# One PSUM read per tile in the cosine layer, and rounds of part-array matmuls issued as one piece

## The chip, the cores and the metric

The kernel runs on one core of a Trainium2 chip. The metric is device time in microseconds (us) of one execution. TensorE (PE) does matmuls, VectorE (DVE), ScalarE (ACT) and GpSimd (POOL) the elementwise work, and SyncE (SP) issues the transfers between HBM and SBUF. Matmul results land in PSUM, which has 8 banks here: four stand as accumulators, four are a ring that all other matmul results share.

## The reference

Shapes: q, k, v are 8 x 8 x 576 x 64, p is 8 x 8 x 32 x 64, the two layers have d_model 512 and d_ff 2048, and 4608 tokens.

```
def sm_attn(qq, kk, vv):
    s = scale * qq @ kk.T
    a = exp(s - max(s)); a = a / (sum(a) + 1e-9)
    return a @ vv
p_packed = sm_attn(p, k, v)             # per batch and head, 32 packed rows
x = sm_attn(q, p_packed, p_packed)      # then heads side by side: 4608 x 512
h = x @ w_in;   x = (h * cos(h)) @ w_out                       # layer 1
h = x @ w_in2;  out = (h * tanh(softplus(h))) @ w_out2         # layer 2
```

## The kernel before, in words

The program has two stages. Stage 1 (to about 843 us) does the attention and layer 1 together, stage 2 does layer 2 with fewer products (a Strassen-like scheme) and is not touched.

**Layer 1** goes through 256 steps n, a tile of 288 tokens by 128 hidden units each (16 token tiles `t`, 16 hidden tiles `s`). `l1(n)` takes a bank of the ring and does six matmuls into it (`mm3` twice: each product is done as hi*hi, hi*lo, lo*hi, hence lines 145, 146 and 147 of every matmul row). `chain_first(n)` and `chain_cos(n)` make g = h*cos(h); `chain_split(n)` makes g's high part (rounded, L819) and low part (the rest, L822 on POOL); `l2(n)` multiplies them with w_out into four accumulator banks, 12 matmuls. `evac(t)` writes a finished token tile to HBM. The chain reads `st["h"]`, the bank of `l1`, three times: on ACT at L802 (the whole number of turns, written as int32), on DVE at L804 (h minus that many turns) and on DVE at L812 (times h). Between them L805 clamps the angle on DVE and L811 takes the sine on ACT. The bank goes back to the ring when L812 is done.

**The attention** runs beside it as units with stages that a table places at steps: `k_unit` (16 of them, packed keys), `q_unit` (16, one per token tile) and `w_unit` (40, which fold the packed values into w_in). Their matmuls have 32 output columns, so each uses a part of the array: eight of them (L218 in `k_unit.s2_pe`, L351 in `q_unit.s2_pe`, L491 in `w_unit.pe`; there four where a unit has one batch) fill all parts and are called a round here, and `k_unit.s5_pe` (L279) has twenty. An fp32 matmul leaves two records in the trace, so a round of eight shows as x16.

**Order.** Instructions are written step by step, but a list scheduler at build time sets the order on each engine from priorities and a timeline of its own. On the chip an engine takes its instructions in that order, and one that waits holds all behind it. `tc.high_priority(offset=...)` lifts an instruction in the scheduler's queue, `tc.issue_after(ins)` keeps it behind `ins`. Before, `w_unit.pe` alone uses both to pull the rest of a round up behind its first matmul.

Of the kernel before, what the change touches and what calls it, by code (L numbers as in the profile page):

```python
# [8 lines left out]
F32 = mybir.dt.float32  # L9
F32R = mybir.dt.float32r  # L10
I32 = mybir.dt.int32
AF = mybir.ActivationFunctionType
ALU = mybir.AluOpType
AX = mybir.AxisListType

B, H, S, D, NPK = 8, 8, 576, 64, 32
DM, DFF = 512, 2048
NTOK = B * S
TT = 288
# [3 lines left out]
NBT = NTOK // BT  # L23
LAG_A = 3
G_MOD = 2
G_ACT = (0, 1)
C_MOD = 2
C_POOL = ()
W_POS = ((57, 1.1), (55, 1.2), (52, 1.2))
K_LD = 3  # L30
Q_LD = 2
# [22 lines left out]
Q_DVE = (0, 0, 0)  # L54
X2_AT = 231
COMB = 240
STOP = 0
W0E = (-3, 5, -1, 9)
K0_G1 = 1
# [9 lines left out]
HP_W = 400  # L69
# [13 lines left out]
TWO_PI = 2.0 * math.pi  # L83
STEP = [None]
PERM = ((0, 2, 1, 3), (1, 3, 0, 2))


def build(tc, q, k, v, p, w1i, w1o, w2i, w2o, out):
    nc = tc.nc
    ctx = ExitStack()  # L90
    with ctx:
        wpool = ctx.enter_context(tc.tile_pool(name="wpool", bufs=1))
# [5 lines left out]
        def nm(s):  # L98
            cnt[0] += 1
            return f"{s}_{cnt[0]}"  # L100
# [17 lines left out]

        ident = wpool.tile([128, 128], F32, name="ident")
        make_identity(nc, ident)  # L120
        halfpi = wpool.tile([128, 1], F32, name="halfpi")
        nc.vector.memset(halfpi, math.pi / 2)
        quarter = wpool.tile([128, 1], F32, name="quarter")
        nc.vector.memset(quarter, 0.25)
        wpool.tile([128, 8], F32, name="gap_w")
# [6 lines left out]
        ap = apool_cm.__enter__()  # L132
# [22 lines left out]
        def trans2(dst, raw):  # L155
# [2 lines left out]
                bass.AP(raw.tensor, raw.offset, [raw.ap[0], [544, 2], [64, 9], [1, 32]]),  # L158
            )

        PK = {}
        lastexp = [None]

        def k_unit(b, g, alloc_v):
# [16 lines left out]
            def vload(i):  # L181
                def f():
                    r = alloc_v([128, 512])
                    if i < 2:
                        h = 4 * g + 2 * i
                        nc.sync.dma_start(
                            r.rearrange("p (h w) -> p h w", h=2),
                            v[b, h : h + 2, :512, :].rearrange("h (t c) d -> t h (c d)", c=4),
                        )
                    else:  # L190
                        nc.sync.dma_start(
                            r[:64, :256].rearrange("p (h d) -> p h d", d=D),
                            v[b, 4 * g : 4 * g + 4, 512:576, :].rearrange("h s d -> s h d"),
                        )
                    st["vr"].append(r)

                return f
# [14 lines left out]

            def s2_pe():
                st["s1"] = [ring() for _ in range(2)]
                for l in range(4):
                    h = PERM[par][l]
                    for x in range(2):
                        nc.tensor.matmul(  # L218
                            st["s1"][x][32 * l : 32 * l + 32, :TT].rearrange("p (s a) -> p a s", a=9),
                            st["pp"][64 * x : 64 * x + 64, 32 * h : 32 * h + 32],  # L220
                            st["kt"][64 * x : 64 * x + 64, TT * h : TT * h + TT].rearrange("p (a s) -> p a s", s=32),
                            start=True,
                            stop=True,
                        )

            def s2_ew():
                sm = ap.tile([128, 8], F32, tag="sm", bufs=3, name=nm("sm"))
# [20 lines left out]
            def s4_pe():  # L248
                e = st["e"]
                t1, t2 = ring(), ring()  # L250
                ev = e[:, :512].rearrange("p (t c) -> p c t", c=4)
                for c in range(4):
                    nc.tensor.transpose(t1[:, 128 * c : 128 * c + 128], ev[:, c], ident)
                nc.tensor.transpose(t2[:64, :128], e[:, 512:576], ident)
                st["t"] = (t1, t2)

            def s4_ew():
                t1, t2 = st["t"]
                a4 = tmp_tile([128, 512])
                a5 = ap.tile([128, 128], F32, tag="a5", bufs=1, name=nm("a5"))  # L260
                nc.scalar.copy(a4, t1)
                nc.scalar.copy(a5[:64], t2[:64, :128])
                st["a"] = (a4, a5)
                sm = st["sm"]
                nc.vector.tensor_tensor(sm[:, 6:7], sm[:, 4:5], sm[:, 5:6], ALU.add)
                nc.vector.tensor_scalar(sm[:, 6:7], sm[:, 6:7], EPS, None, ALU.add)
                nc.vector.reciprocal(sm[:, 7:8], sm[:, 6:7])

            def s5_pe():
                a4, a5 = st["a"]  # L270
                ps = ring()
                for c in range(5):
                    n = 128 if c < 4 else 64
                    a = a4[:, 128 * c : 128 * c + 128] if c < 4 else a5[:64]
                    for l in range(4):
                        h = PERM[par][l]
                        vr = st["vr"][h // 2] if c < 4 else st["vr"][2]
                        o = 256 * (h % 2) + D * c if c < 4 else D * h
                        nc.tensor.matmul(  # L279
                            ps[32 * l : 32 * l + 32, :D],  # L280
                            a[:, 32 * l : 32 * l + 32],
                            vr[:n, o : o + D],
                            start=c == 0,
                            stop=c == 4,
                        )
                st["pv"] = ps

            def s5_ew():
# [28 lines left out]
        def q_unit(t, pre=None):  # L317
# [27 lines left out]

            def s2_pe():
                st["s"] = [ring() for _ in range(2)]
                for l in range(4):
                    h = PERM[b % 2][l]
                    for g in range(2):  # L350
                        nc.tensor.matmul(  # L351
                            st["s"][g][32 * l : 32 * l + 32, :TT],
                            PK[(b, g)][64 * g : 64 * g + 64, 32 * l : 32 * l + 32],
                            st["kt"][64 * g : 64 * g + 64, TT * h : TT * h + TT],
                            start=True,
                            stop=True,
                        )

            def s2_ew():
                sq = tmp_tile([128, 2, TT])  # L360
# [120 lines left out]
        def w_unit(bs, fg, g, ms):  # L481
            st = {}

            def pe():
                for b in bs:
                    st[b] = ring()

                def head(b, l):
                    h = PERM[b % 2][l]
                    r = 64 * (h % 2)  # L490
                    return nc.tensor.matmul(  # L491
                        st[b][32 * l : 32 * l + 32],
                        PK[(b, g)][r : r + 64, 32 * l : 32 * l + 32],
                        ms[h // 2]["m"][r : r + 64],
                        start=True,
                        stop=True,
                    )

                todo = sorted(((b, l) for b in bs for l in range(4)), key=lambda x: (-(PERM[x[0] % 2][x[1]] // 2), -x[0]))
                ins = head(*todo[0])  # L500
                with tc.issue_after(getattr(ins, "ins", ins)), tc.high_priority(offset=HP_W):
                    for x in todo[1:]:
                        head(*x)

            def ew():
                for b in bs:
                    w = W1.get((b, fg))
                    if w is None:
                        w = W1[(b, fg)] = wab_tile(b % 2, [128, 2, 2, 512], F32R)
                    nc.scalar.copy(w[:, g, 0], st[b])  # L510
                    nc.vector.tensor_tensor(w[:, g, 1], st[b], w[:, g, 0], ALU.subtract)

            return pe, ew
# [284 lines left out]

        def chain_first(n):
            st = hst[n]  # L800
            ki = ap.tile([128, TT], I32, tag="ki", bufs=2, name=nm("ki"))
            nc.scalar.activation(ki, st["h"], AF.Identity, bias=quarter, scale=1.0 / TWO_PI)  # L802
            r = ap.tile([128, TT], F32, tag="r", bufs=4, name=nm("r"))
            nc.vector.scalar_tensor_tensor(r, ki, -TWO_PI, st["h"], ALU.mult, ALU.add)  # L804
            (nc.gpsimd if n % C_MOD in C_POOL else nc.vector).tensor_scalar(r, r, 1.570796, -4.712388, ALU.min, ALU.max)  # L805
            st["r"] = r

        def chain_cos(n):
            st = hst[n]
            g = st["r"]  # L810
            nc.scalar.activation(g, g, AF.Sin, bias=halfpi, scale=1.0)  # L811
            nc.vector.tensor_tensor(g, g, st["h"], ALU.mult)  # L812
            st["g"] = g

        def chain_split(n):
            st = hst[n]
# [20 lines left out]
        def evac(t):  # L837
            for dc in range(4):
                o = ap.tile([128, TT], F32, tag="xo", bufs=3, name=nm("xo"))
                x = acc[t][dc][:, :TT].rearrange("p (a s) -> p s a", s=32)  # L840
                y = o.rearrange("p (s a) -> p s a", s=32)
                if dc % 2 == 0:
                    nc.scalar.copy(y, x)
                else:
                    nc.vector.tensor_copy(y, x)
                nc.sync.dma_start(x2d[t][:, dc, :], o)

        X = {}
# [351 lines left out]
```

## Time and profile before

| | |
|---|---|
| median of 3 runs | 1555.14 us (1553.41 to 1558.32) |
| the profiled execution | 1555.48 us, of which the span of instructions is 1552.9 us |
| PE busy, share of the span | 1475.9 us, 95% |
| DVE, ACT, POOL busy | 72%, 57%, 41% |
| granted PE clock, mean over the span | 0.989 of full speed |

A PE that is busy is not a PE at its peak: matmuls overlap, so what a piece of the matmul stream costs is read from start to start in the timeline, not from busy time. The idle time that a row names stands behind its last bar, with what ended it.

### The profile page before, as it was taken

How to read it: one execution, taken by the hardware profiler on the slowest of the kernel's cores; microseconds unless marked ns; L12 is line 12 of the kernel's file. 1: busy time of each engine (PE TensorE's matmuls, PEld its weight loads, DVE VectorE, ACT ScalarE, POOL GpSimd, SP SyncE). 2: the span in 40 equal slices, each digit the busy share in tenths (PEclk: the TensorE clock that was granted, in tenths of full speed). 3: DMA queues.
4: the chain of work that ended last, by engine and by line, in shares of the span. 5: the costliest groups of instructions: out<-in, count | busy, mean ns of one | idle time of the engine just before them, and what ended most of it. 6: DMA issues, size and time to landing. Idle time of an engine off the chain costs nothing.

```text
span 1552.9 us, 28652 instructions
## 1 busy us (share of the span) xinstructions
PE 1475.9 (95%) x9728; PEld 1278.3 (82%) x9728; DVE 1117.8 (72%) x2082; ACT 883.9 (57%) x1838; POOL 639.2 (41%) x634
## 2 busy tenths in 40 slices
PE   3789999999999999999999999999999999999998
PEld 1567778788987898788999887888889898888997
DVE  4896666777776877678675878678668857766756
ACT  3675767666667677667665455344443534454443
POOL 0462333245643544627754666223522622352102
PEclk9899999999999999999999999999999999999999
DMA  9889676436648457533313767668868877877887
GB/s 293 283 214 226 170 184 161 123 101 176 186 122 225 139 152 195 163 107 104 104 49 98 259 217 241 193 196 242 266 212 235 298 223 219 244 205 221 241 257 202
DMA packets 247377, 300.75 MB, mean 194 GB/s; under 512 B 104384, under 2 KB 129472, under 8 KB 247232
## 3 DMA queue, kind: packets, MB, share of 16 engines
q1 hardware_dynamic: 246432, 298.73, 66.1%
q8 instruction: 77, 1.26, 0.3%
q14 instruction: 68, 0.56, 0.1%
q10 hardware_dynamic: 800, 0.20, 0.1%
HBM read 242.22 MB, written 56.62 MB: 192 GB/s over the span
## 4 chain that ended last, share of the span: by engine, by line
PE 50%; DVE 6%; ACT 3%; issue 2%; DMA 2%; POOL 1%; SPq 0%; DVEq 0%; ACTq 0%; POOLq 0%
PE acc L146 9%; PE acc L147 9%; PE acc L145 9%; PE ps L145 8%; PE ps L147 8%; PE ps L146 8%; DVE r L805 1%; ACT r L811 1%; DVE r L812 1%; DVE r L804 1%; DMA raw<-in_moe_w_in_dram 1%; DVE wab L897 1%; ACT wab L896 1%; PE ps L491 0%; DMA tst<-wt 0%
## 5 line engine op out<-in xcount | busy, mean ns | idle before, releaser
L822 POOL TENSOR_TENSOR gh<-r,gh 128x288 fp32r<-128x288 f32 x256 | 214.9, 847 | 334.3 <-ACT gh L819 231.7
L146 PE MATMUL acc<-gh,wo 128*128 128x288 f32 x1024 | 301.5, 301 | 2.2 <-POOL gh L822 1.7
L147 PE MATMUL acc<-gh,wo 128*128 128x288 f32 x1024 | 298.2, 298 | 0.0
L955 POOL TENSOR_TENSOR gh<-t,gh 128x512 fp32r<-128x512 f32 (+1 forms) x108 | 144.2, 1340 | 351.5 <-ACT gh L954 290.7
L145 PE MATMUL acc<-gh,wo 128*128 128x288 f32 x1024 | 273.7, 304 | 2.1 <-ACT gh L819 1.9
L145 PEld LDWEIGHTS acc<-gh,wo 128*128 128x128 f32 x1024 | 181.2, 190 | 34.6 <-issue 11.9
L146 PE MATMUL acc<-gh,T 128*128 128x512 f32 (+1 forms) x560 | 207.0, 371 | 2.2 <-DVE gh L955 1.7
L145 PE MATMUL ps<-wab,ws 128*128 128x512 f32 (+1 forms) x560 | 206.0, 369 | 1.8 <-ACT gh L954 0.8
L146 PEld LDWEIGHTS acc<-gh,wo 128*128 128x128 f32 x1024 | 194.1, 190 | 15.9 <-issue 9.5
L146 PE MATMUL ps<-wab,ws 128*128 128x512 f32 (+1 forms) x560 | 206.4, 369 | 0.0
L147 PE MATMUL ps<-wab,ws 128*128 128x512 f32 (+1 forms) x560 | 205.4, 369 | 0.0
L147 PE MATMUL acc<-gh,T 128*128 128x512 f32 (+1 forms) x560 | 205.1, 369 | 0.0
L147 PEld LDWEIGHTS acc<-gh,wo 128*128 128x128 f32 x1024 | 194.2, 190 | 5.8 <-issue 5.6
L955 DVE TENSOR_TENSOR gh<-wo,gh 128x512 fp32r<-128x512 f32 (+1 forms) x160 | 128.7, 810 | 81.7 <-ACT gh L954 81.3
L811 ACT ACTIVATE r<-r,halfpi 128x288 f32<-128x288 f32 x256 | 136.3, 535 | 83.9 <-DVE r L805 81.6
L145 PE MATMUL acc<-gh,T 128*128 128x512 f32 (+1 forms) x560 | 181.9, 369 | 0.6 <-DMA T<-tst 0.5
L145 PE MATMUL ps<-aT,wab 128*128 128x288 f32 x512 | 159.7, 312 | 22.7 <-DVE r L812 16.5
L812 DVE TENSOR_TENSOR r<-r,ps 128x288 f32<-128x288 f32 x256 | 114.5, 449 | 73.3 <-ACT r L811 72.5
L802 ACT ACTIVATE ki<-ps,quarter 128x288 int32<-128x288 f32 x256 | 125.1, 496 | 59.7 <-PE ps L147 49.6
L804 DVE SCALAR_TENSOR_TENSOR r<-ki,ps 128x288 f32<-128x288 int32 x256 | 113.8, 447 | 55.8 <-ACT ki L802 39.5
L146 PE MATMUL ps<-aT,wab 128*128 128x288 f32 x512 | 152.2, 297 | 0.0
L147 PE MATMUL ps<-aT,wab 128*128 128x288 f32 x512 | 151.5, 296 | 0.0
(169 smaller groups left out, 2956.1 us busy)
## 6 DMA issues: line engine op xcount, KB each, us to landing
T<-tst SPq DMA_DIRECT2D x280, 256.0 KB, 3.1
ws<-wst SPq DMA_DIRECT2D x224, 256.0 KB, 3.0
ld<-ws SPq DMA_DIRECT2D x80, 256.0 KB, 3.5
kr<-in_k_dram SPq DMA_DIRECT2D x64, 272.0 KB, 5.6
kr<-in_q_dram SPq DMA_DIRECT2D x60, 272.0 KB, 6.0
tst<-wt SPq DMA_DIRECT2D x56, 256.0 KB, 2.6
wst<-ws SPq DMA_DIRECT2D x56, 256.0 KB, 2.5
x2d<-xo SPq DMA_DIRECT2D x64, 144.0 KB, 1.8
```

What stands on the lines that cost most here:

```text
L145: nc.tensor.matmul(ps, l0, r0, start=first, stop=False, skip_group_check=more)
L146: nc.tensor.matmul(ps, l0, r1, start=False, stop=False, skip_group_check=more)
L147: nc.tensor.matmul(ps, l1, r0, start=False, stop=last, skip_group_check=more)
L802: nc.scalar.activation(ki, st["h"], AF.Identity, bias=quarter, scale=1.0 / TWO_PI)
L804: nc.vector.scalar_tensor_tensor(r, ki, -TWO_PI, st["h"], ALU.mult, ALU.add)
L805: (nc.gpsimd if n % C_MOD in C_POOL else nc.vector).tensor_scalar(r, r, 1.570796, -4.712388, ALU.min, ALU.max)
L811: nc.scalar.activation(g, g, AF.Sin, bias=halfpi, scale=1.0)
L812: nc.vector.tensor_tensor(g, g, st["h"], ALU.mult)
L822: nc.gpsimd.tensor_tensor(gh[:, 1], st["g"], gh[:, 0], ALU.subtract)
L896: nc.scalar.copy(x[:, a, 0, :n], src)
L897: (nc.gpsimd if k % 2 == 0 else nc.vector).tensor_tensor(x[:, a, 1, :n], src, x[:, a, 0, :n], ALU.subtract)
L955: eng.tensor_tensor(hl[:, 1, :n], src, hl[:, 0, :n], ALU.subtract)
```

## The change

Three things are changed. In the chain, ACT copies h / 2pi out of PSUM into an SBUF tile `f`; everything after it works on `f` and a second SBUF tile `u` (turns as int32, angle in turns, sine). The clamp is gone, the product is f * sin, and `evac` multiplies by 2pi. The high part is made by ACT at even steps and by DVE at odd ones (`G_ACT`), before by ACT at all. In the rounds, a new helper `rounds` puts a 128x32 matmul (with the identity as weights) on the round's first bank, reading the end of the round's last operand, ahead of the first part-array matmul, and lifts the others behind that. It serves `k_unit.s2_pe`, `q_unit.s2_pe` and those `w_unit.pe` that have two batches; `k_unit.s5_pe` uses it without the short matmul and starts with the block that was last. To that end the small transpose and its copy move from partitions 0 to 63 to 64 to 127.

```diff
-G_ACT = (0, 1)
+G_ACT = (0,)
+HOLD_N = 32
+        def rounds(banks, src, first, rest):
+            for ps in banks:
+                nc.tensor.matmul(ps[:, :HOLD_N], ident, src[:, :HOLD_N], start=True, stop=True)
+            with tc.high_priority(offset=HP_W):
+                ins = first()
+            with tc.issue_after(getattr(ins, "ins", ins)), tc.high_priority(offset=HP_W):
+                for f in rest:
+                    f()
...
+                todo = [lambda x=x, l=l: head(x, l) for x, l in sorted(((x, l) for x in range(2) for l in range(4)), key=lambda y: (-PERM[par][y[1]], -y[0]))]
+                rounds(st["s1"][:1], st["kt"][:, 1152 - HOLD_N :], todo[0], todo[1:])
...
-                nc.tensor.transpose(t2[:64, :128], e[:, 512:576], ident)
+                nc.tensor.transpose(t2[:, :128], e[:, 448:576], ident)
...
-                nc.scalar.copy(a5[:64], t2[:64, :128])
+                nc.scalar.copy(a5[64:], t2[64:, :128])
...
+                todo = [lambda c=c, l=l: head(c, l) for c in (4, 0, 1, 2, 3) for l in range(4)]
+                rounds((), None, todo[0], todo[1:])
...
-                ins = head(*todo[0])
-                with tc.issue_after(getattr(ins, "ins", ins)), tc.high_priority(offset=HP_W):
-                    for x in todo[1:]:
-                        head(*x)
+                rounds([st[b] for b in bs[:-1]], ms[1]["m"], lambda: head(*todo[0]), [lambda x=x: head(*x) for x in todo[1:]])
...
-            ki = ap.tile([128, TT], I32, tag="ki", bufs=2, name=nm("ki"))
-            nc.scalar.activation(ki, st["h"], AF.Identity, bias=quarter, scale=1.0 / TWO_PI)
-            r = ap.tile([128, TT], F32, tag="r", bufs=4, name=nm("r"))
-            nc.vector.scalar_tensor_tensor(r, ki, -TWO_PI, st["h"], ALU.mult, ALU.add)
-            (nc.gpsimd if n % C_MOD in C_POOL else nc.vector).tensor_scalar(r, r, 1.570796, -4.712388, ALU.min, ALU.max)
-            st["r"] = r
+            f = st["f"] = ap.tile([128, TT], F32, tag="f", bufs=4, name=nm("f"))
+            nc.scalar.activation(f, st["h"], AF.Identity, scale=1.0 / TWO_PI)
+            u = st["u"] = ap.tile([128, TT], F32, tag="u", bufs=2, name=nm("u"))
+            ki = u.bitcast(I32)
+            nc.scalar.activation(ki, f, AF.Identity, bias=quarter)
+            nc.vector.scalar_tensor_tensor(u, f, 0.25, ki, ALU.add, ALU.subtract)
...
-            g = st["r"]
-            nc.scalar.activation(g, g, AF.Sin, bias=halfpi, scale=1.0)
-            nc.vector.tensor_tensor(g, g, st["h"], ALU.mult)
-            st["g"] = g
+            f, u = st["f"], st["u"]
+            nc.scalar.activation(u, u, AF.Sin, scale=6.283185)
+            nc.vector.tensor_tensor(f, f, u, ALU.mult)
+            st["g"] = f
...
-                    nc.scalar.copy(y, x)
+                    nc.scalar.mul(y, x, TWO_PI)
```

In `q_unit.s2_pe` the edit is the same as in `k_unit.s2_pe`. Two places show what it does to the order. The first is PE at the last `k_unit`; `kt_7825` is its keys, `ps_7838` and `ps_7839` the two banks of the round. Before:

```order
L147 MATMUL acc_7630<-gh_7742,wo_626 128x288
L218 MATMUL ps_7838<-kt_7825,pp_7823 32x9x32
L218 MATMUL ps_7839<-kt_7825,pp_7823 32x9x32
L145 MATMUL ps_7881<-aT_7340,wab_6209 128x288
L146 MATMUL ps_7881<-aT_7340,wab_6209 128x288
L147 MATMUL ps_7881<-aT_7340,wab_6209 128x288
L145 MATMUL ps_7881<-aT_7340,wab_6209 128x288
L146 MATMUL ps_7881<-aT_7340,wab_6209 128x288
L147 MATMUL ps_7881<-aT_7340,wab_6209 128x288
L218 MATMUL ps_7838<-kt_7825,pp_7823 32x9x32
L218 MATMUL ps_7839<-kt_7825,pp_7823 32x9x32
```

The same round now (`kt_7867`, banks `ps_7880` and `ps_7881`; the short matmul is L161):

```order
L145 MATMUL acc_7671<-gh_7725,wo_582 128x288
L161 MATMUL ps_7880<-kt_7867,ident 128x32
L225 MATMUL ps_7881<-kt_7867,pp_7865 32x9x32
L225 MATMUL ps_7880<-kt_7867,pp_7865 32x9x32
L225 MATMUL ps_7881<-kt_7867,pp_7865 32x9x32
L225 MATMUL ps_7880<-kt_7867,pp_7865 32x9x32
L225 MATMUL ps_7881<-kt_7867,pp_7865 32x9x32
L225 MATMUL ps_7880<-kt_7867,pp_7865 32x9x32
L225 MATMUL ps_7881<-kt_7867,pp_7865 32x9x32
L225 MATMUL ps_7880<-kt_7867,pp_7865 32x9x32
L143 MATMUL ps_7924<-aT_7381,wab_6243 128x288
```

Six matmuls of layer 1 stood inside the round (two of its eight ahead of them, six behind); they now stand behind it, and the short matmul ahead of it.

The second place is ACT at the first steps of layer 1, where weights are still being prepared (L436, L450 and L510 before, L452, L466 and L523 now). Before:

```order
L802 ACTIVATE ki_457<-ps_443,quarter 128x288
L811 ACT_TABLE_LOAD
L811 ACTIVATE r_391<-r_391,halfpi 128x288
L436 ACTIVATE wab_373<-wab_373 128x512
L811 ACTIVATE r_422<-r_422,halfpi 128x288
L510 CAST wab_394<-ps_450 128x512
L436 ACTIVATE tmp_584<-raw_482 128x512
L819 CAST gh_425<-r_391 128x288
L802 ACTIVATE ki_509<-ps_484,quarter 128x288
```

Now:

```order
L818 ACTIVATE u_393<-f_391,quarter 128x288
L818 ACTIVATE u_424<-f_422,quarter 128x288
L815 ACTIVATE f_459<-ps_445 128x288
L452 ACTIVATE wab_375<-wab_375 128x512
L523 CAST wab_396<-ps_452 128x512
L824 ACT_TABLE_LOAD
L824 ACTIVATE u_393<-u_393 128x288
L452 ACTIVATE tmp_586<-raw_484 128x512
L824 ACTIVATE u_424<-u_424 128x288
L815 ACTIVATE f_511<-ps_486 128x288
L452 ACTIVATE tmp_632<-raw_534 128x512
L832 CAST gh_427<-f_391 128x288
```

The read of the next bank (`ps_445`, before `ps_443`) still stands ahead of the first sine, but the bank is now free after it, and the read of `ps_486` stands ahead of the first high part where that of `ps_484` stood behind it.

## Rows read from the trace of the kernel before

**Rows 1.** Busy time by stretch: length, busy us of each engine, clock, DMA share.

```profile
60.00:120.00 60.00, 50.58 (x369) 41.46 (x368) 55.64 (x105) 45.15 (x90) 35.44 (x31) 0.91 0.87 246
120.00:840.00 720.00, 696.61 (x5772) 608.99 (x5761) 510.57 (x1150) 488.68 (x1066) 333.61 (x381) 0.99 0.54 145
```

**Rows 2.** Timeline of PE: a K round in two pieces (start, us, instruction, count).

```profile
593.96 0.29 PE L147 MATMUL acc<-gh,wo 128*128 128x288 f32 x1
594.18 0.68 PE L218 MATMUL ps<-kt,pp 64*32 64x288 f32 x4
...
595.02 0.29 PE L146 MATMUL ps<-aT,wab 128*128 128x288 f32 x1
```

**Rows 3.** Timeline of PE: a K round in one piece.

```profile
494.47 0.72 PE L218 MATMUL ps<-kt,pp 64*32 64x288 f32 x16
```

**Rows 4.** Timeline of PE: half a W round, and a whole one.

```profile
648.52 0.29 PE L147 MATMUL acc<-gh,wo 128*128 128x288 f32 x1
648.74 1.06 PE L491 MATMUL ps<-ld,pk 64*32 64x512 f32 x8
...
649.98 0.29 PE L146 MATMUL acc<-gh,wo 128*128 128x288 f32 x1
...
655.91 1.09 PE L491 MATMUL ps<-ld,pk 64*32 64x512 f32 x16
```

**Rows 5.** Timeline of PE: two matmuls of L279 alone.

```profile
552.62 0.29 PE L147 MATMUL ps<-aT,wab 128*128 128x288 f32 x1
552.85 0.30 PE L279 MATMUL ps<-ld,tmp 128*32 128x64 f32 x4
...
553.32 0.29 PE L146 MATMUL ps<-aT,wab 128*128 128x288 f32 x1
```

**Rows 6.** Timeline of PE: one full-array fp32 matmul between those of layer 1.

```profile
516.84 0.29 PE L147 MATMUL acc<-gh,wo 128*128 128x288 f32 x1
516.97 0.27 PE L297 MATMUL ps<-ident,pxw 128*128 128x128 f32 x1
...
517.21 0.29 PE L146 MATMUL ps<-aT,wab 128*128 128x288 f32 x1
```

**Rows 7.** PE by line: busy, mean ns of one; idle before, and what ended it.

```profile
L146 PE MATMUL acc<-gh,wo 128*128 128x288 f32 x1024 | 301.5, 301 | 2.2 <-POOL gh L822 1.7
...
L145 PE MATMUL acc<-gh,wo 128*128 128x288 f32 x1024 | 273.7, 304 | 2.1 <-ACT gh L819 1.9 <-ACT xo L843 0.2
...
L145 PE MATMUL ps<-aT,wab 128*128 128x288 f32 x512 | 159.7, 312 | 22.7 <-DVE r L812 16.5 <-ACT a L262 2.6 <-DVE wab L511 2.2
...
L351 PE MATMUL ps<-kt,pk 64*32 64x288 f32 x256 | 20.1, 431 | 2.0 <-DVE r L812 1.8 <-ACT tmp L238 0.2
```

**Rows 8.** Timeline of PE: the longest wait for a bank.

```profile
54.81 0.61 PE L145 MATMUL ps<-aT,wab 128*128 128x288 f32 x1 [6.22 <-DVE r L812]
```

**Rows 9.** DVE by line, the whole span.

```profile
L805 DVE TENSOR_SCALAR r<-r 128x288 f32<-128x288 f32 x256 | 123.7, 487 | 4.9
L812 DVE TENSOR_TENSOR r<-r,ps 128x288 f32<-128x288 f32 x256 | 114.5, 449 | 73.3 <-ACT r L811 72.5
L804 DVE SCALAR_TENSOR_TENSOR r<-ki,ps 128x288 f32<-128x288 int32 x256 | 113.8, 447 | 55.8 <-ACT ki L802 39.5 <-POOL gh L822 14.4 <-POOL wt L596 0.5
```

**Rows 10.** DVE by line: one PSUM source, and two SBUF sources, same shape.

```profile
L1086 DVE TENSOR_TENSOR t<-wo,wo 128x512 f32<-128x512 f32 (+1 forms) x120 | 101.6, 852 | 14.1 <-POOL gh L955 12.8
L1012 DVE TENSOR_TENSOR wo<-ps,u 128x512 f32<-128x512 f32 (+1 forms) x120 | 74.7, 629 | 45.7 <-PE ps L147 45.3
```

**Rows 11.** ACT by line, the whole span.

```profile
L811 ACT ACTIVATE r<-r,halfpi 128x288 f32<-128x288 f32 x256 | 136.3, 535 | 83.9 <-DVE r L805 81.6 <-DVE r L812 0.9
L802 ACT ACTIVATE ki<-ps,quarter 128x288 int32<-128x288 f32 x256 | 125.1, 496 | 59.7 <-PE ps L147 49.6 <-DVE r L804 9.3
L819 ACT CAST gh<-r 128x288 fp32r<-128x288 f32 x256 | 108.4, 428 | 47.5 <-DVE r L812 27.5 <-PE acc L147 15.0 <-DVE kt L156 2.0
...
L843 ACT COPY xo<-acc 128x288 f32<-128x288 f32 x32 | 12.2, 394 | 7.9 <-PE acc L147 7.9
```

More of the change, by code (lines that the diff above doesn't have):

```diff
@@ L25 @@
 G_MOD = 2
-G_ACT = (0, 1)
-C_MOD = 2
-C_POOL = ()
+G_ACT = (0,)
 W_POS = ((57, 1.1), (55, 1.2), (52, 1.2))
@@ L120, in build @@
         make_identity(nc, ident)
-        halfpi = wpool.tile([128, 1], F32, name="halfpi")
-        nc.vector.memset(halfpi, math.pi / 2)
+        wpool.tile([128, 1], F32, name="gap_h")
         quarter = wpool.tile([128, 1], F32, name="quarter")
@@ L191, in f @@
                         nc.sync.dma_start(
-                            r[:64, :256].rearrange("p (h d) -> p h d", d=D),
+                            r[64:, :256].rearrange("p (h d) -> p h d", d=D),
                             v[b, 4 * g : 4 * g + 4, 512:576, :].rearrange("h s d -> s h d"),
@@ L214, in s2_pe, with head @@
                 st["s1"] = [ring() for _ in range(2)]
-                for l in range(4):
+                def head(x, l):
                     h = PERM[par][l]
[L217 to L224, printed above, removed]
+                    return nc.tensor.matmul(
+                        st["s1"][x][32 * l : 32 * l + 32, :TT].rearrange("p (s a) -> p a s", a=9),
+                        st["pp"][64 * x : 64 * x + 64, 32 * h : 32 * h + 32],
+                        st["kt"][64 * x : 64 * x + 64, TT * h : TT * h + TT].rearrange("p (a s) -> p a s", s=32),
+                        start=True,
+                        stop=True,
+                    )
+                todo = [lambda x=x, l=l: head(x, l) for x, l in sorted(((x, l) for x in range(2) for l in range(4)), key=lambda y: (-PERM[par][y[1]], -y[0]))]
+                rounds(st["s1"][:1], st["kt"][:, 1152 - HOLD_N :], todo[0], todo[1:])
             def s2_ew():
@@ L271, in s5_pe, with head @@
                 ps = ring()
[L272 to L285, printed above, removed]
+                def head(c, l):
+                    r = slice(0, 128) if c < 4 else slice(64, 128)
+                    a = a4[:, 128 * c : 128 * c + 128] if c < 4 else a5
+                    h = PERM[par][l]
+                    vr = st["vr"][h // 2] if c < 4 else st["vr"][2]
+                    o = 256 * (h % 2) + D * c if c < 4 else D * h
+                    return nc.tensor.matmul(
+                        ps[32 * l : 32 * l + 32, :D],
+                        a[r, 32 * l : 32 * l + 32],
+                        vr[r, o : o + D],
+                        start=c == 4,
+                        stop=c == 3,
+                    )
+                todo = [lambda c=c, l=l: head(c, l) for c in (4, 0, 1, 2, 3) for l in range(4)]
+                rounds((), None, todo[0], todo[1:])
                 st["pv"] = ps
@@ L347, in s2_pe, with head @@
                 st["s"] = [ring() for _ in range(2)]
-                for l in range(4):
+                def head(g, l):
                     h = PERM[b % 2][l]
[L350 to L357, printed above, removed]
+                    return nc.tensor.matmul(
+                        st["s"][g][32 * l : 32 * l + 32, :TT],
+                        PK[(b, g)][64 * g : 64 * g + 64, 32 * l : 32 * l + 32],
+                        st["kt"][64 * g : 64 * g + 64, TT * h : TT * h + TT],
+                        start=True,
+                        stop=True,
+                    )
+                todo = [lambda g=g, l=l: head(g, l) for g, l in sorted(((g, l) for g in range(2) for l in range(4)), key=lambda y: (-PERM[b % 2][y[1]], -y[0]))]
+                rounds(st["s"][:1], st["kt"][:, 1152 - HOLD_N :], todo[0], todo[1:])
             def s2_ew():
@@ L842, in evac @@
                 if dc % 2 == 0:
-                    nc.scalar.copy(y, x)
+                    nc.scalar.mul(y, x, TWO_PI)
                 else:
-                    nc.vector.tensor_copy(y, x)
+                    nc.vector.tensor_scalar(y, x, TWO_PI, None, ALU.mult)
                 nc.sync.dma_start(x2d[t][:, dc, :], o)
```

## The prediction

> **What bounds the kernel now.** I read the stretches first. From 120 to 840 us, where layer 1 and the attention run together, PE is busy 696.6 of 720 us, DVE 510.6 and ACT 488.7 [rows 1]: the matmul stream sets the pace there, and the others have slack of 209 and 231 us. From 60 to 120 us it is otherwise: DVE is busy 55.6 of 60 us and PE 50.6, at a mean granted clock of 0.91 [rows 1]. Stage 2, after that, keeps its code, and its order on PE stays what it was; I leave it out. So two things count: what PE's stream is made of, and what it waits for. Busy time does not show the first, because matmuls overlap, so I went to PE's timeline and read starts. Full-array matmuls of layer 1 start 0.13 us apart (516.84 to 516.97 [rows 6]). For the second I read PE's waits by line [rows 7, 8].
>
> **Rounds in pieces.** A piece is an unbroken run of part-array matmuls. From the last full matmul ahead of a piece to the second one behind it stand 593.96 to 595.02, 1.06 us [rows 2]; without the piece that would be two steps of 0.13. So this piece, two matmuls of a K round, costs 0.80 us. A whole round of eight runs 0.72 us, the two alone 0.68 [rows 2, 3]: the array does all parts at once, and a piece costs the same whatever is in it. The same for W: half a round costs 649.98 - 648.52 - 0.26 = 1.20 us, and runs 1.06 us where a whole one runs 1.09 [rows 4]. For the packed products (L279) two matmuls alone cost 553.32 - 552.62 - 0.26 = 0.44 us [rows 5]; more of them add their own time, but that is there in any case, so 0.44 is the price of a cut.
>
> The order on PE gives the counts. Before there are 116 such runs: 22 hold matmuls of K rounds (16 rounds), 27 of Q (16), 49 of W (40) and 27 of L279 (16), nine runs holding two kinds. Now there are 82: 16, 16, 39 and 16, five with two kinds. So 6 and 11 pieces at 0.80 go (4.8 and 8.8 us; Q has K's shape), 10 at 1.20 (12.0) and 11 at 0.44 (4.8), in all 30.4. A run with two kinds saves one change between full array and parts; there are four fewer, about 0.3 each, so 29 us are left. Bounds: 34 runs at 0.44 or at 1.20 each, 15 to 41 us. All of it is time of PE's own stream, so it comes off the end wherever PE sets the pace.
>
> **The short matmuls.** 16 K, 16 Q and 24 W rounds get one, 56 in all. The trace has no 128x32 fp32 matmul. The nearest row is the full-array fp32 transpose at 516.97, which costs 517.21 - 516.84 - 0.26 = 0.11 us [rows 6], for one record; an fp32 matmul leaves two, each with its load of 128 columns of weights, so 0.22 us and 12.3 us in all. From below, the loads could hide and it costs nothing; from above, it is as dear as the smallest cut of the stream, 0.44 us [rows 5], or 25 us. I take 12.3, because the transpose is the nearest form by far.
> The Trainium skill, TensorEngine Tiling (Array Packing), section Instruction Overhead, says a matmul has a floor of some 60 cycles whatever its free size. By that alone a pass would be 25 ns and the 56 an estimated 2.8 us, and the sum 9.5 us lower; no row here shows a matmul that short, and the row for 128 columns is at four times that.
>
> **The bank goes back early.** PE waited 16.5 us in layer 1's first products and 1.8 in Q rounds for L812, the chain's last read of a bank [rows 7]; 6.2 of that is one wait at 54.81 us [rows 8]. Now the first ACT read frees the bank, so these waits lose their cause. What is late next is that ACT read itself, queued behind other ACT work. Of the 12.1 us later on I count 10 as gone. Of the 6.2 I count 3, because the DVE that was slow there has the same weights to prepare, and PE needs those too. Together 13 us; bounds 0 and 18.
>
> **The chain's new durations.** DVE: the clamp goes (487 ns, L805). The two others ran 447 and 449 ns with one source in PSUM [rows 9]; both now read two SBUF tiles. The trace has that on another line: of the same 128x512 operation, 629 ns with a PSUM source and 852 with two SBUF sources, while POOL was at work beside it in part of the cases [rows 10]. I add that 220 ns to each: 2 x 670. Half the steps have the high part on DVE, a one-source SBUF operation like the clamp, 244 ns per step. Together 1583 in place of 1383 ns, 0.20 us more per step. ACT: a PSUM read without a bias tile costs 394 (L843), the turns from SBUF with one 535 (as L811), the sine without one 428 (as L819), half a copy 214, together 1571 in place of 535 + 496 + 428 = 1459, 0.11 us more per step [rows 11]. Some 20 of the 256 steps fall before 120 us, 236 behind: there DVE gains 47 us and ACT 26, which makes 558 and 515 of 720 us, still behind PE. In the DVE-bound first part 20 steps at 0.20 cost 4 us. The chain's results are late for PE 2.2 + 2.1 us now [rows 7]; with a longer chain but more steps of layer 1 run ahead in the order, I let that double, 4 us more. Bounds for both together: 0 (all of it is hidden) to 30 us (0.12 us per step).
>
> **Nothing else.** evac keeps its count and kind with a factor added, the wider transpose has the same weights' columns, and SP's transfers are the same.
>
> **Sum.** 1555.5 (the profiled execution, 0.3 above the median) - 29 + 12.3 - 13 + 4 + 4 = 1533.8, so 1534 us.
>
> **Rivals.** *DVE becomes the bound.* The chain's two DVE operations now read two SBUF tiles, and POOL's low part (L822) reads SBUF at the same time; where each waits for the other, the operations double. For it: 852 against 629 ns, and the clamp's mean of 487 for work smaller than its neighbours' [rows 9, 10]. Against: DVE has 209 us free over 236 steps, 0.89 us a step [rows 1], of which my sum uses 0.20. It decides when the two together cost 0.69 more than I have, from about 1.0 us each on. Then what PE saves no longer counts: at 1.05 each DVE is 0.07 us a step over the pace of now, 17 us, so 1572.
> [...]
> *The holds stall.* The short matmul stops PE's queue until the round's last operand and first bank are there, with all of layer 1 behind it, where before a part could start. At 0.35 us for each of 56, 20 us, the gain is eaten: about 1553. Against: PE's waits at L351 were only 2.0 us for 16 rounds [rows 7], and work for the stream stands ahead of each in the order.
> *More comes back.* All waits for L812 go, the short matmul hides, nothing is late: 1555.5 - 29 - 18 = 1508 at most, about 1517 with half of it.
>
> **How the numbers follow.** My forecast 0.66, more back 0.15, holds stall 0.11, DVE bound 0.08. A change of 0.3% (4.7 us) is about what a measurement here can tell. The forecast's own range, from the bounds of its terms, is 1522 to 1546; taking in most of the others, 1517 to 1551. Faster: the first two and a little of the third, 0.83; same 0.08; slower 0.09.
>
> **What would show it.** Right: no K or Q round in PE's timeline shorter than x16, pieces at the same 0.8 and 1.2 us; the short matmul's start to start with its neighbours near 0.22 us more; no wait for the product line among PE's waits on ring banks; the two DVE lines near 670 ns. Wrong: PE waits at the short matmuls' line over 10 us, PE's idle time before 120 us longer, DVE above 85% of the stretch from 120 us to layer 1's end, or waits for `gh` on PE of tens of us.

## The result, and the profile after

The change makes the kernel slower: 1576.32 us (median of 5 runs, 1572.05 to 1578.12) against 1554.44, a ratio of 1.0134 with a 95% interval of 1.0113 to 1.0155. The forecast was 1534 us, faster. The profiled execution took 1572.05 us, its span is 1569.5. It is the fastest of the five, so the two profiles are 16.6 us apart where the medians are 21.9 apart.

Two stretches of layer 1 first (length, then busy us of PE, weight loads, DVE, ACT and POOL, then clock and DMA):

```profile
60.00:120.00 60.00, 48.93 (x366) 40.70 (x365) 54.70 (x98) 46.59 (x99) 37.13 (x32) 0.92 0.84 247
120.00:840.00 720.00, 673.36 (x5732) 607.07 (x5731) 528.10 (x1014) 512.65 (x1161) 346.97 (x371) 0.99 0.53 144
```

In the 720 us PE is busy 23 us less than before, though the engines beside it still have 192 and 207 us free [rows 1]. Nothing is full, and yet PE runs less. Its waits by line (L143 and L144 are the first and second of three products, L161 the short matmuls, L310 the last transpose of a `k_unit`; busy, mean ns of one, idle before it and what ended that):

```profile
L144 PE MATMUL acc<-gh,wo 128*128 128x288 f32 x1024 | 303.9, 300 | 9.1 <-POOL gh L835 8.9
L143 PE MATMUL acc<-gh,wo 128*128 128x288 f32 x1024 | 289.8, 302 | 13.6 <-DVE xo L858 6.0 <-DVE gh L834 5.2 <-ACT gh L832 2.1
L143 PE MATMUL ps<-aT,wab 128*128 128x288 f32 x512 | 164.9, 322 | 17.0 <-ACT f L815 9.2 <-ACT tmp L248 3.2 <-ACT wab L523 1.7
...
L161 PE MATMUL ps<-kt,ident 128*128 128x32 f32 x64 | 11.1, 256 | 16.5 <-DVE kt L154 16.5
L310 PE MATMUL ps<-ident,pxw 128*128 128x128 f32 x16 | 5.0, 311 | 8.7 <-DVE pxw L303 8.7
```

Where L812 was waited for 16.5 us there are now 9.2 for the ACT read. The waits for the chain's results, `gh`, went from 1.7 + 1.9 to 8.9 + 5.2 + 2.1 us [rows 7]. The other 6.0 at L143 are for `xo`, DVE's copy of a finished accumulator bank, and L310's 8.7, 3.1 before, are for DVE too. The 16.5 at L161 are the start: two waits before 19 us, where L218 waited 11.7 and 4.5 before.

The elementwise engines, DVE, ACT and POOL (L819 the angle, L825 the product, L834 the high part on DVE, L835 the low part):

```profile
L835 POOL TENSOR_TENSOR gh<-f,gh 128x288 fp32r<-128x288 f32 x256 | 227.2, 892 | 307.3 <-DVE gh L834 141.6
...
L819 DVE SCALAR_TENSOR_TENSOR u<-f,u 128x288 f32<-128x288 f32 x256 | 166.4, 658 | 49.0 <-ACT u L818 48.0
L825 DVE TENSOR_TENSOR f<-f,u 128x288 f32<-128x288 f32 x256 | 151.0, 595 | 65.3 <-ACT u L824 62.0
...
L824 ACT ACTIVATE u<-u 128x288 f32<-128x288 f32 x256 | 112.3, 443 | 90.5 <-DVE u L819 89.3
L815 ACT ACTIVATE f<-ps 128x288 f32<-128x288 f32 x256 | 102.8, 405 | 38.9 <-POOL gh L835 25.7 <-PE ps L145 12.2
```

The two DVE operations went from 447 and 449 to 658 and 595 ns [rows 9], and ACT's read of the bank, which is to set the bank free, waits 25.7 us for POOL: the tile f goes back only when the low part is done. One place shows where the time of an operation goes, DVE's timeline first, then POOL's:

```profile
571.93 1.04 DVE L819 SCALAR_TENSOR_TENSOR u<-f,u 128x288 f32<-128x288 f32 x1 [0.65 <-ACT u L818]
572.89 1.08 DVE L595 TENSOR_SCALAR raw<-raw 128x512 int32<-128x512 int32 x1
573.89 0.45 DVE L819 SCALAR_TENSOR_TENSOR u<-f,u 128x288 f32<-128x288 f32 x1
```

```profile
571.85 0.80 POOL L835 TENSOR_TENSOR gh<-f,gh 128x288 fp32r<-128x288 f32 x1
572.61 1.07 POOL L615 TENSOR_TENSOR raw<-raw 128x256 f32<-128x256 f32 x1
```

DVE starts L819 0.08 us after POOL's low part and needs 1.04 us; with POOL free at 573.89 it needs 0.45. The same holds over the whole trace, as counted from the records of three runs (e5 is an experiment below):

| DVE operation, sources | no POOL instruction beside it | POOL busy all through |
|---|---|---|
| L819 after, two in SBUF | 450 ns (97 cases, 461 at most) | 940 ns (52) |
| L825 after, two in SBUF | 453 ns (115, 461 at most) | 955 ns (34) |
| L820 in e5, one in PSUM, one in SBUF | 451 ns (80) | 451 ns (99) |
| L826 in e5, one in PSUM, one in SBUF | 451 ns (122) | 450 ns (67) |
| the clamp L805 before, one in SBUF | 305 ns (107) | 664 ns (68) |

So an operation with two SBUF sources is no slower by itself: its mean of 658 or 595 ns is a mix of 0.45 us and of waits behind POOL. The clamp, with one source in SBUF, waits as well; the operations with a PSUM source do not.

To weigh this against the rounds, I added up PE's records from layer 1's first matmul to stage 2's first. The columns are idle time, the steps from start to start that touch a part-array, fp32 or short matmul, and the steps from full matmul to full matmul.

| us | idle | part-array, fp32, short | full to full | sum |
|---|---|---|---|---|
| before | 39.2 | 137.2 | 624.4 | 800.8 |
| after | 60.9 | 119.3 | 637.4 | 817.5 |

The middle column is 17.9 us shorter. With fewer pieces 33 more steps go from full to full, at 0.13 us 4.3 of the last column's growth, so by the forecast's count, which takes off two such steps for each piece, the rounds gained 13.6 where 29 less 12.3 makes 16.7. Idle time grew by 21.7 us, all of it after 120 us, and the full matmuls by 13.0. Some 4 more of that last are the clock (288 steps of over 0.2 us where there were 247): after a long wait the next full matmuls start 0.24 us apart in place of 0.13, as here, where the granted clock of 721 to 725 us is 0.57, in the main the lower of the two levels:

```profile
721.55 0.61 PE L143 MATMUL ps<-aT,wab 128*128 128x288 f32 x1 [3.37 <-ACT f L815]
721.96 0.45 PE L144 MATMUL ps<-aT,wab 128*128 128x288 f32 x1
722.20 0.45 PE L145 MATMUL ps<-aT,wab 128*128 128x288 f32 x1
```

A round now, for comparison with the pieces [rows 2, 3], then a short matmul that landed among full ones:

```profile
602.58 0.29 PE L145 MATMUL acc<-gh,wo 128*128 128x288 f32 x1
602.72 0.30 PE L161 MATMUL ps<-kt,ident 128*128 128x32 f32 x2
602.95 0.71 PE L225 MATMUL ps<-kt,pp 64*32 64x288 f32 x16
603.59 0.40 PE L143 MATMUL ps<-aT,wab 128*128 128x288 f32 x1
...
499.75 0.29 PE L145 MATMUL acc<-gh,wo 128*128 128x288 f32 x1
499.88 0.30 PE L161 MATMUL ps<-ld,ident 128*128 128x32 f32 x2
500.02 0.38 PE L143 MATMUL acc<-gh,wo 128*128 128x288 f32 x1
500.23 0.29 PE L144 MATMUL acc<-gh,wo 128*128 128x288 f32 x1
```

Ahead of a round it costs 602.95 - 602.58 = 0.37 us where the step into a piece was 594.18 - 593.96 = 0.22 [rows 2], so 0.15; among full matmuls 500.23 - 499.75 - 0.26 = 0.22, the forecast's figure. Of the 56, 33 stand ahead of a round in this way and 7 among full matmuls. Estimated from the some 60 cycles a matmul that the Trainium skill (TensorEngine Tiling (Array Packing), Instruction Overhead) states, at 2.4 GHz, a pass would take 25 ns; the rows here make it 75 to 110.

### The profile page after: what moved, and what is told of

Same layout as the page of the kernel before. It is cut to its first block, busy times and chain, and to the rows that moved or that the text cites. A ratio compares the mean times of both kernels' runs of the same rounds, so it can differ in the third digit from the quotient of the medians.

```text
span 1569.5 us, 28655 instructions
## 1 busy us (share of the span) xinstructions
PE 1471.0 (94%) x9840; PEld 1295.4 (83%) x9840; DVE 1144.0 (73%) x1953; ACT 920.4 (59%) x1968; POOL 663.8 (42%) x634
## 4 chain that ended last, share of the span: by engine, by line
PE 53%; DVE 12%; ACT 8%; DMA 5%; issue 4%; POOL 3%; SPq 0%; DVEq 0%; ACTq 0%; POOLq 0%
PE acc L144 9%; PE acc L145 9%; PE acc L143 9%; PE ps L143 8%; PE ps L144 8%; PE ps L145 8%; DVE u L819 3%; DVE f L825 3%; DMA raw<-in_moe_w_in_dram 2%; POOL gh L835 2%; ACT u L824 1%; ACT f L815 1%; ACT u L818 1%; PE ps L507 1%; DVE kt L154 1%
## 5 line engine op out<-in xcount | busy, mean ns | idle before, releaser
L835 POOL TENSOR_TENSOR gh<-f,gh 128x288 fp32r<-128x288 f32 x256 | 227.2, 892 | 307.3 <-DVE gh L834 141.6
L144 PE MATMUL acc<-gh,wo 128*128 128x288 f32 x1024 | 303.9, 300 | 9.1 <-POOL gh L835 8.9
L143 PE MATMUL acc<-gh,wo 128*128 128x288 f32 x1024 | 289.8, 302 | 13.6 <-DVE xo L858 6.0
L145 PE MATMUL acc<-gh,wo 128*128 128x288 f32 x1024 | 300.2, 297 | 0.0
L144 PE MATMUL acc<-gh,T 128*128 128x512 f32 (+1 forms) x560 | 207.1, 371 | 2.2 <-DVE gh L968 1.6
L143 PEld LDWEIGHTS acc<-gh,wo 128*128 128x128 f32 x1024 | 188.2, 191 | 24.1 <-DVE gh L834 6.4
L144 PEld LDWEIGHTS acc<-gh,wo 128*128 128x128 f32 x1024 | 195.0, 190 | 15.0 <-POOL gh L835 14.6
L143 PE MATMUL ps<-wab,ws 128*128 128x512 f32 (+1 forms) x560 | 206.0, 369 | 0.5 <-DVE wo L1025 0.4
L144 PE MATMUL ps<-wab,ws 128*128 128x512 f32 (+1 forms) x560 | 206.4, 369 | 0.0
L819 DVE SCALAR_TENSOR_TENSOR u<-f,u 128x288 f32<-128x288 f32 x256 | 166.4, 658 | 49.0 <-ACT u L818 48.0
L825 DVE TENSOR_TENSOR f<-f,u 128x288 f32<-128x288 f32 x256 | 151.0, 595 | 65.3 <-ACT u L824 62.0
L145 PEld LDWEIGHTS acc<-gh,wo 128*128 128x128 f32 x1024 | 194.5, 190 | 1.3 <-issue 1.3
L143 PE MATMUL acc<-gh,T 128*128 128x512 f32 (+1 forms) x560 | 181.9, 369 | 0.7 <-ACT gh L967 0.7
L143 PE MATMUL ps<-aT,wab 128*128 128x288 f32 x512 | 164.9, 322 | 17.0 <-ACT f L815 9.2
L824 ACT ACTIVATE u<-u 128x288 f32<-128x288 f32 x256 | 112.3, 443 | 90.5 <-DVE u L819 89.3
L144 PE MATMUL ps<-aT,wab 128*128 128x288 f32 x512 | 155.0, 303 | 0.0
L145 PE MATMUL ps<-aT,wab 128*128 128x288 f32 x512 | 154.4, 303 | 0.0
L143 PEld LDWEIGHTS ps<-aT,wab 128*128 128x128 f32 x512 | 99.6, 195 | 53.6 <-ACT f L815 16.1
```

Of the source, the lines that this page charges most:

```text
L143: nc.tensor.matmul(ps, l0, r0, start=first, stop=False, skip_group_check=more)
L144: nc.tensor.matmul(ps, l0, r1, start=False, stop=False, skip_group_check=more)
L145: nc.tensor.matmul(ps, l1, r0, start=False, stop=last, skip_group_check=more)
L819: nc.vector.scalar_tensor_tensor(u, f, 0.25, ki, ALU.add, ALU.subtract)
L824: nc.scalar.activation(u, u, AF.Sin, scale=6.283185)
L825: nc.vector.tensor_tensor(f, f, u, ALU.mult)
```

## The experiments

Theory 1: the chain costs the time; 1a by its tiles, which come free late, 1b by two-SBUF operations on DVE that wait for POOL, 1c by ACT's extra operation. Theory 2: the rounds cost it, since a short matmul holds PE's queue. The ratio sets every median beside the kernel before on the same chip, in five rounds each; there that kernel took 1554.42 us for e1 to e4, 1555.90 for e5 to e8 and 1557.55 for e9 and e10.

| run | what it is | us | ratio to before, 95% interval |
|---|---|---|---|
| e1_rounds | rounds alone | 1552.27 | 0.9979 (0.9966 to 0.9992) |
| e2_chain | chain alone | 1573.69 | 1.0117 (1.0096 to 1.0139) |
| e3_f5 | change, five f tiles | 1574.17 | 1.0112 (1.0092 to 1.0132) |
| e4_psum | rounds, chain from PSUM, no clamp | 1539.80 | 0.9891 (0.9870 to 0.9912) |
| e5_src | change, DVE sources turned back to PSUM | 1544.26 | 0.9921 (0.9906 to 0.9937) |
| e6_two_sbuf | e4, one product from SBUF | 1546.89 | 0.9941 (0.9926 to 0.9956) |
| e7_old_rounds | e4's chain, rounds as before | 1545.78 | 0.9936 (0.9919 to 0.9953) |
| e8_no_short | e4 without short matmuls | 1547.14 | 0.9946 (0.9930 to 0.9962) |
| e9_act_all | e4, high parts all on ACT | 1542.74 | 0.9909 (0.9882 to 0.9937) |
| e10_after_act_all | change, high parts all on ACT | 1562.80 | 1.0041 (1.0022 to 1.0060) |

**The two halves.** e1 has the rounds of the change and the chain, constants and `evac` of before; e2 the reverse.

```diff
 # e1_rounds, against the changed kernel
-G_ACT = (0,)
+G_ACT = (0, 1)
-            f = st["f"] = ap.tile([128, TT], F32, tag="f", bufs=4, name=nm("f"))
-            nc.scalar.activation(f, st["h"], AF.Identity, scale=1.0 / TWO_PI)
...
+            nc.scalar.activation(ki, st["h"], AF.Identity, bias=quarter, scale=1.0 / TWO_PI)
+            r = ap.tile([128, TT], F32, tag="r", bufs=4, name=nm("r"))
...
```

> The rounds of the change alone, with the chain of the kernel before (three PSUM reads, clamp, high part on ACT). Theory 1, the chain is the loss (its two-SBUF DVE operations wait for POOL, and its tiles come free late): the rounds keep their own gain, 29 us of pieces less 12 of short matmuls, so 1555 - 17 = 1538 us. Theory 2, the rounds are the loss (a short matmul holds PE's queue until operand and bank are there): 1560 us or more, with PE's waits grown as in the changed kernel.

```diff
 # e2_chain, against the changed kernel (rounds as before, for K, Q, W and L279)
-                rounds(st["s1"][:1], st["kt"][:, 1152 - HOLD_N :], todo[0], todo[1:])
+                for l in range(4):
+                    for x in range(2):
...
```

> The chain of the change alone, with the rounds of the kernel before. Theory 1: the whole loss and the rounds' gain beside it, 1576 + 17 = 1593 us, with PE waiting for gh some 15 us. Theory 2: the bank comes back early and nothing else changes, 1545 us or less.

The chain is the loss: it costs 19 us alone. The rounds do no harm, so theory 2 falls, but they bring 2 us and not 17, and with that e2 missed the 1593 us that theory 1 had for it. The shorter stream is there (117.4 us in the middle column, 19.8 less than before, 17 by the forecast's count), but idle time rose from 39.2 to 53.7 us and took most of it back; e1's first products:

```profile
L146 PE MATMUL ps<-aT,wab 128*128 128x288 f32 x512 | 162.7, 318 | 32.0 <-DVE r L828 30.5 <-ACT aT L412 0.6 <-ACT tmp L274 0.5
```

L828 is L812 of before: 30.5 us of waits for the bank where there were 16.5 [rows 7].

**The ring of f.**

```diff
-            f = st["f"] = ap.tile([128, TT], F32, tag="f", bufs=4, name=nm("f"))
+            f = st["f"] = ap.tile([128, TT], F32, tag="f", bufs=5, name=nm("f"))
```

> The changed kernel with five f tiles in place of four. Theory 1a, the ring of f is what is late (f is taken by the first ACT read now and given back by POOL's low part, so ACT waits for POOL and keeps the bank): ACT's 26 us of waits at the f line fall to under 12 and the time to 1565 us or less. Theory 1b, the DVE operations' waits for POOL are what is late: within 4 us of 1576. Theory 2: the same.

```profile
L815 ACT ACTIVATE f<-ps 128x288 f32<-128x288 f32 x256 | 102.9, 405 | 34.6 <-POOL gh L835 23.1 <-PE ps L145 10.5
```

The waits at the f line fell from 38.9 to 34.6 us, those for POOL from 25.7 to 23.1, and not to under 12; the time fell by 2 us, within the runs' spread. More than five tiles were not tried. So theory 1a falls as far as a fifth tile can show: the wait at f is there, but one more tile doesn't cure what makes POOL and DVE late.

**The sources.** e4 reads PSUM three times, without a clamp:

```diff
-            f = st["f"] = ap.tile([128, TT], F32, tag="f", bufs=4, name=nm("f"))
-            nc.scalar.activation(f, st["h"], AF.Identity, scale=1.0 / TWO_PI)
...
+            nc.scalar.activation(ki, st["h"], AF.Identity, bias=quarter, scale=1.0 / TWO_PI)
+            nc.vector.scalar_tensor_tensor(u, st["h"], 1.0 / TWO_PI, ki, ALU.mult, ALU.subtract)
...
+            nc.scalar.activation(u, u, AF.Sin, bias=halfpi, scale=6.28318)
+            nc.vector.tensor_tensor(u, u, st["h"], ALU.mult)
```

> The changed kernel with a chain that has no clamp but reads PSUM three times: turns on ACT, h/2pi minus turns on DVE from PSUM, sine with a bias, product with h from PSUM; high part half on DVE as in the change; evac as before. So each DVE operation has one SBUF source, and the bank is held to the product. Theory 1b: the two DVE operations are back at 450 ns and the time is that of the rounds alone or less, 1530 to 1538 us. Theory 1a: also under 1550, since the tile is taken by DVE as before, but ACT then has no waits for POOL. Theory 2: 1560 us or more.

1539.80 us, the fastest of all here, just above the 1530 to 1538 expected. It changes several things at once, so e5 turns back the DVE sources and what goes with them: the sine's bias tile and `evac`'s plain copy.

```diff
-            nc.vector.scalar_tensor_tensor(u, f, 0.25, ki, ALU.add, ALU.subtract)
+            nc.vector.scalar_tensor_tensor(u, st["h"], 1.0 / TWO_PI, ki, ALU.mult, ALU.subtract)
...
-            nc.scalar.activation(u, u, AF.Sin, scale=6.283185)
-            nc.vector.tensor_tensor(f, f, u, ALU.mult)
+            nc.scalar.activation(u, u, AF.Sin, bias=halfpi, scale=6.28318)
+            nc.vector.tensor_tensor(f, u, st["h"], ALU.mult)
```

> The changed kernel with one thing turned back: the two DVE operations of the chain read h from PSUM again where they read f (the angle as h/2pi minus turns, the product as sine times h; the sine gets its bias back, evac its plain copy). ACT still makes f and takes the turns from it, and the f tile is held as before, so ACT's work, the tiles' lives and the rounds stay; only the second SBUF source goes, and the bank is held to the product again. Theory 1b, the two-SBUF sources cost the time (they wait for POOL and POOL for them): the two lines fall from 658 and 595 ns to 450, and the time to 1550 us or less, though the bank comes late. Theory 1c, the cost is ACT's third operation per step and the longer hold of f: within 5 us of 1576 or above, since the early bank is lost too.

1544.26 us, 32 less than the change, with ACT's three operations, the f ring and the rounds kept, and the early bank given up. ACT even has more to do, since the sine with its bias tile takes 533 ns in place of 443. Its lines on DVE, POOL and ACT:

```profile
L826 DVE TENSOR_TENSOR f<-u,ps 128x288 f32<-128x288 f32 x256 | 114.6, 450 | 86.6 <-ACT u L825 80.9 <-POOL gh L836 2.3 <-ACT u L819 1.1
L820 DVE SCALAR_TENSOR_TENSOR u<-ps,u 128x288 f32<-128x288 f32 x256 | 114.2, 451 | 68.4 <-ACT u L819 67.5
...
L836 POOL TENSOR_TENSOR gh<-f,gh 128x288 fp32r<-128x288 f32 x256 | 214.2, 841 | 319.9 <-ACT gh L833 141.2 <-DVE gh L835 121.6 <-issue 17.2
...
L816 ACT ACTIVATE f<-ps 128x288 f32<-128x288 f32 x256 | 102.4, 403 | 59.7 <-PE ps L146 45.2 <-POOL gh L836 13.1
```

450 and 451 ns again, the low part 841 in place of 892, and ACT's read of the bank waits for PE now (45.2) and less for POOL (13.1). So theory 1b is shown, up to what the new order of the instructions adds (see what stays open). Theory 1c, ACT's extra operation, has the 4 to 5 us between e5 and e4 at most, and their intervals overlap.

```diff
 # e6_two_sbuf, against e4
-            nc.vector.tensor_tensor(u, u, st["h"], ALU.mult)
+            nc.vector.tensor_tensor(u, u, u, ALU.mult)
```

> The chain that reads PSUM three times without a clamp (e4), but its product reads two SBUF tiles: u times u in place of u times h, so h is left out of the result. The instruction count is that of e4, and the bank comes back one operation and one ACT pass earlier. Theory 1b: the product line goes from 450 to some 600 ns, POOL's low part gets longer, and the time is 1545 us or more although the bank is back early. Theory 3, the bank's return is what sets the pace: under 1536 us, less than e4.

One product from SBUF (u times u, so h is left out of the result) costs 7 us, though it frees the bank one ACT pass and one DVE operation sooner. PE's first products wait 10.2 us for the bank in place of 13.1, not enough to pay for it. The product's line in e6, and then in e4:

```profile
L824 DVE TENSOR_TENSOR u<-u 128x288 f32<-128x288 f32 x256 | 157.1, 617 | 69.3 <-ACT u L823 68.5
```

```profile
L824 DVE TENSOR_TENSOR u<-u,ps 128x288 f32<-128x288 f32 x256 | 114.1, 449 | 73.2 <-ACT u L823 72.1
```

**The rounds with a shorter chain.** e7 is e4's chain with the rounds of before (the edit of e2), e8 is e4 with empty lists of banks in `rounds`.

> The chain of e4 with the rounds of the kernel before. With e4 it tells what whole rounds are worth when the chain is short. Where PE's stream sets the pace with e4, the rounds are worth the 20 us that their pieces less the short matmuls measured in e1's trace, and this takes 1555 to 1560 us. Where the ring of banks still sets it, they are worth 2 us as in e1, and this takes 1542 us.

```diff
 # e8_no_short, against e4 (the same for Q and W)
-                rounds(st["s1"][:1], st["kt"][:, 1152 - HOLD_N :], todo[0], todo[1:])
+                rounds((), st["kt"][:, 1152 - HOLD_N :], todo[0], todo[1:])
```

> e4 without the 56 short matmuls; the rounds keep their order by the lifted rest. If the rounds fall into pieces again without it, the time is some 1550 us; if they stay whole, the 12 us that the short matmuls take from PE's stream come back, in part, 1530 to 1538 us.

Whole rounds are worth 6 us here (e7, between its two expectations) and 2 with the old chain (e1), less than they take off the middle column, 11 and 20 us. Without the short matmuls part-array work falls into 117 runs in place of 84 (half of the K rounds and most Q rounds are split), the middle column goes from 117.3 to 138.5 us, and the time up by 7. So with their own price in it they save the stream 21 us, and idle time (43.4 in e4, 31.2 in e8) takes back more than half.

**Who is late, DVE or ACT.** In both e9 and e10 the one edit is the constant:

```diff
-G_ACT = (0,)
+G_ACT = (0, 1)
```

> e4 with the high parts all on ACT again, as in the kernel before; beside e1 only the clamp is then gone. If the clamp was what kept the bank (DVE's 487 ns of a two-port operation in the middle of the chain), this has most of e4's gain over e1's 1552: 1540 to 1543 us. If e4's gain came from the even split of the high parts, this is near 1550. The split's own price: DVE's copies cost 466 ns each in contention with POOL, against 428 on ACT, so this could also beat e4.

> The changed kernel with the high parts all on ACT again. If DVE is what is late (two-SBUF operations in the queue with POOL), 128 fewer DVE operations of 472 ns help: 1568 us or less. If ACT is what is late (three operations per step and its waits for f slots), 128 more ACT operations of 426 ns make it slower than 1576.

In the changed kernel it wins 13 us, although ACT gets 128 more operations of 426 ns: DVE is what is late there. In e4, where DVE has no contended operation but the copies, e9 shows no difference clear of the intervals. Beside e1, e9 lacks the clamp alone: the clamp is worth some 10 us (9.5 between the medians, 11 by the ratios). The change had left the clamp out too, so the rest of its chain lost this gain and 19 us more.

## Why the prediction was wrong

**Rounds in pieces, and the short matmuls: right as terms.** 29 less 12.3, that is 16.7 us, were forecast; by the same count 13.6 were measured on the stream, and 17 in e1. That "all of it is time of PE's own stream, so it comes off the end wherever PE sets the pace" was not right: e1 shows 2 us off the end. PE was busy 97% of the stretch, but it stood just ahead of the ring of four banks; when the stream got shorter, it ran into the ring (30.5 us of waits for L812's successor). With the clamp gone and half the high parts on DVE the same wait is 13.1 us in e4, and the rounds are worth 6:

```profile
L144 PE MATMUL ps<-aT,wab 128*128 128x288 f32 x512 | 160.5, 314 | 16.0 <-DVE u L824 13.1 <-DVE wab L525 1.3 <-ACT tmp L272 0.8
```

**The chain's new durations: the step that failed.** The durations were well sized as means: 2 x 670 ns forecast, 658 and 595 measured; DVE at 528 of 720 us where 558 were forecast. What failed is what I made of them: "still behind PE", hence 4 + 4 us, where e2 measured 19 us of loss for the chain as a whole, gains included. I set busy time against free time, and made 1.0 us an operation the point from which it decides. But a step goes over DVE twice and over ACT three times in turn, each engine takes its queue in order, and a late angle holds the sine, everything behind the sine on ACT, and so the next read of a bank. A mean also hides that single operations take from 0.4 to 1.7 us. Worked out from the changed kernel's records, the k-th of each line paired: from the start of a bank's last product to ACT's read are 4.26 us, where before there were 1.52, and to the end of the low part 12.4 in place of 9.2; so most of the delay is ahead of ACT's read. e5 puts 32 us on the sources, and e10 shows that taking work off DVE's queue wins 13 of them back.

**The bank goes back early: failed with it.** By the same pairing, from the start of its last product to the end of the read that frees it, a bank was held 5.90 us and is held 4.67, 1.2 less, and not the three DVE operations and the sine, 1.9 us of work [rows 9, 11], that no longer stand ahead of its return; the read that frees it now stands behind ACT's waits. The waits for it went from 16.5 to 9.2, and those for `gh` grew from 3.6 to 16.2 us, against the 4 that I allowed.

**The rivals.** The first was the right mechanism with the wrong threshold: the Trainium skill's rule (SBUF, State Buffer, Who interferes with whom) that two SBUF sources on DVE contend with a GpSimd operation that reads SBUF holds here in both directions, 450 against 658 and 595 ns on DVE and 841 against 892 on POOL. Its time, 1572, is near the measured 1576 by luck: it needed 1.05 us an operation and a full DVE, and DVE was busy 528 of 720 us. That holds stall was not it: e1 is not slower than before, and after the start PE waited 3.4 us at the short matmuls' line in the change.

**The range and the signs.** The range of 1522 to 1546 was called one from the bounds of the terms, but the bad bounds together give 1555.5 - 15 + 25 + 30 = 1595, so it was narrower than its terms; and half of the way from 1534 to 1508 is 1521, not 1517. The signs did not tell right from wrong either: no K or Q round is in pieces, no wait for the product line stands on a ring bank, and the two DVE lines are near 670 ns, as the right forecast was to show. Of the signs of being wrong, the 20 us at the short matmuls' line are mostly the start, DVE stands at 73% of the stretch, and only the waits for `gh`, 16 us, point at the cause.

**What stays open.** The scheduler makes a new order for each kernel, so a difference of two runs holds some of that: between the change and e5, 72% of the places in PE's order hold the same kind of instruction, between the change and e3 94%. e5's 32 us and e6's 7 point one way, and the line means agree, but how much is order was not separated. Nor was it tried to lengthen the ring of banks, since all eight are used.

## What to carry to other kernels

Before moving a DVE operation's operand from PSUM to SBUF, ask what GpSimd does at that time: a PSUM source ran 450 ns here whether GpSimd was busy or not, and giving a bank back early by a copy pays only if the engine that copies isn't itself held by the chain. A chain that hops between engines, each of which works through its queue in order, is judged by its latency against the buffers that it holds, not by the busy shares of its engines; where PE stands just ahead of a full ring, time taken out of PE's stream turns into waits until the chain is made shorter too. Here the version that beats both kernels does that: whole rounds, PSUM sources and no clamp, 1539.80 us, 1.1% below the kernel before (0.9 to 1.3%).

## What was not expected of the hardware

A short fp32 matmul of 32 columns on the full array cost 0.22 us among full matmuls, as much as two passes of 128 columns by the forecast's row, but only 0.15 ahead of a part-array round. A DVE operation with two SBUF sources took 450 ns or, with GpSimd busy all through it, 940 to 955 on average, and with a PSUM source 450 either way; the clamp, with a single SBUF source, went from 305 to 664 ns.
